# Windowed attention and a SoLU layer on one core: another order for the opening, two weight blocks' remainders on GpSimd, and the last tile evicted by one engine

## The chip, the core and the metric

The kernel runs on one core of a Trainium2 chip. The metric is device time in microseconds. A core has these engines: TensorE (PE, with its weight loads shown apart as PEld), VectorE (DVE), ScalarE (ACT), GpSimd (POOL) and SyncE (SP), which here only issues DMAs. Each engine works through its own list of instructions in order and waits at semaphores for the others. Matrix products land in PSUM, whose eight banks are one tile here, `banks`.

## What is computed

Attention over 8 batches of 8 heads, 576 positions, 64 wide, with two kinds of masks, and then a layer on the concatenated heads:

```python
mask_plain = (rel >= 0) & (rel < 32)
mask_dil = (rel >= 0) & (rel < 128) & (rel % 4 == 0)
masks = np.stack([mask_plain if h < H // 2 else mask_dil for h in range(H)], axis=0)
scores = np.where(masks[None], scale * (q @ k.T), -1e9)
x = softmax(scores) @ v                       # as 4608 tokens of 512
h = x @ w_in                                  # 512 -> 1024
solu = h * softmax(h)
ln = (solu - mean(solu)) / np.sqrt(var(solu) + 1e-06) * g_ln
out = ln @ w_out                              # 1024 -> 512
```

## The kernel before

**Work.** Attention goes by 32 units n, each two heads of one batch; four units make a batch. The layer goes by 36 tiles i of 128 tokens. Both weights come as 64-bit floating-point numbers and are taken apart on the chip, in 16 blocks b of 128 x 512: blocks 0 to 7 are `w_in` (row group b // 2, column half b % 2), blocks 8 to 15 `w_out`. Every product of the layer is made of three: high part by high part, high part by remainder, remainder by high part.

**Steps.** Each step is a short word with a number. A dictionary at the end of the kernel (`one`) maps words to functions, and the list is the order in which each engine gets its instructions, since scheduling is by hand.

- Loads, all on SP's queue: `q` (one unit's keys and queries, two DMAs), `v` (values), `w` (a block's words, 512 KB, into one of six slots), `i` (the identity, fp32), `ib` (the identity, bf16), `m` (mask), `g` (gains). At most eight loads of a queue are under way: each load waits for the one eight places before it.
- Conversion of block b: `low` and `abs` on ACT (bits out of the words), `sign`, `clamp`, `join` on DVE (the fp32 number), `gain` on ACT (blocks 8 to 15), `hi` on ACT (the rounded high part), and the remainder `lo`. By the letter of `LOW_DIFF` for the block, the remainder is made in one of two ways. With "m" the step `diff` gives TensorE two matmuls of 128 x 512, identity by number and negative identity (`minus`, made once by `neg` on ACT) by high part, and `lo` is a copy by ACT out of PSUM. With "p" `lo` is one subtraction on GpSimd.
- Attention of unit n: `S` (scores on TensorE, for units 0 to 3 with the mask added by a matmul), `mask` (DVE, units from 4 on), `max`, `sub` (DVE for units 0 to 3, GpSimd after), `exp` (ACT), `sum`, `inv`, `norm`, `turn` (DVE), `V` (attend, TensorE), `xh` (ACT spreads the high part into `x_hi`), `xl` (DVE spreads the remainder into `x_lo`; it reads the result of `xh`).
- Layer of tile i: `ha`, `hb`, `hc`, `hd` (24 matmuls of 512 columns into two banks), `peak` (DVE, row maximum), `e` (ACT, exponential), `gate` (DVE, product and row sum), `mid` (centre), `var` (ACT and GpSimd), `t` (transposes on TensorE), `th` (ACT), `tl` (DVE), `o` (24 matmuls), `out` (evict on ACT, store). The two banks of tile i are free for tile i + 1 only after `gate`.

**Order.** `INIT` issues the first loads. `OPENING` is a list written out in words: it interleaves the conversion of all 16 blocks, the first eight units or so and the first tiles. From tile 6 on the fixed list `STEP` takes over. `conv_low` (line 437 of the profile), `conv_abs` (427), `conv_sign` (450), `conv_clamp` (443), `conv_join` (458), `conv_hi` (469), `conv_lo` (482 by ACT, 484 by GpSimd), `spread_hi` (283), `spread_lo` (286), `scores` (191), `attend` (265), `moe_h` (299), `moe_o` (387), `moe_peak` (310) and `moe_gate` (324) are the lines that the rows below name. The last tile is evicted in halves, the left by ACT, the right by DVE (407, 408).

## Time and profile before

| | |
|---|---|
| median of three runs | 567.88 us (567.01 to 571.52) |
| the profiled execution | 567.52 us, of it 565.7 us span of the core's work and 1.8 us around it |
| busy share of the span | PE 94%, PEld 75%, DVE 63%, ACT 42%, POOL 20% |
| mean granted TensorE clock | 0.982 |
| moved by DMA | 51.66 MB, 91 GB/s in the mean |

A row of a timeline gives start, duration (both us), engine, line, operation, written tile <- read tiles, shape and count, and in brackets how long the engine had been idle before it and what ended that. "issue" there means that the profile shows nothing that it waited for. In rows grouped by line the last figures are busy us, mean ns of one, and idle time before with its releaser.

### The profile page before, as it was taken

How to read it: one execution, taken by the hardware profiler on the slowest of the kernel's cores; microseconds unless marked ns; L12 is line 12 of the kernel's file. 1: busy time of each engine (PE TensorE's matmuls, PEld its weight loads, DVE VectorE, ACT ScalarE, POOL GpSimd, SP SyncE). 2: the span in 40 equal slices, each digit the busy share in tenths (PEclk: the TensorE clock that was granted, in tenths of full speed). 3: DMA queues.
4: the chain of work that ended last, by engine and by line, in shares of the span. 5: the costliest groups of instructions: out<-in, count | busy, mean ns of one | idle time of the engine just before them, and what ended most of it. 6: DMA issues, size and time to landing. Idle time of an engine off the chain costs nothing.

```text
span 565.7 us, 16593 instructions
## 1 busy us (share of the span) xinstructions
PE 531.3 (94%) x7424; PEld 422.9 (75%) x7424; DVE 358.2 (63%) x555; ACT 237.3 (42%) x386; POOL 110.6 (20%) x256
## 2 busy tenths in 40 slices
PE   2775799899999999999999999999999999999997
PEld 1443588678888888888888888888888888888885
DVE  2989865576667766567667766567667766533342
ACT  3679754334344333433344333433344333433232
POOL 0002451123112222112112222112112222111111
PEclk9799889899999999999999999999999999999999
DMA  8976102332322233112222222123321000001001
GB/s 304 399 287 237 57 1 93 110 103 93 93 93 92 93 93 93 48 64 93 92 93 93 93 92 93 48 65 93 93 93 48 21 21 21 20 19 38 19 20 37
DMA packets 22103, 51.66 MB, mean 91 GB/s; under 512 B 2704, under 2 KB 3216, under 8 KB 22032
## 3 DMA queue, kind: packets, MB, share of 16 engines
q1 hardware_dynamic: 21888, 50.48, 26.4%
q8 instruction: 58, 0.95, 0.7%
q10 hardware_dynamic: 144, 0.13, 0.1%
q14 instruction: 13, 0.11, 0.1%
HBM read 41.16 MB, written 9.44 MB: 89 GB/s over the span
## 4 chain that ended last, share of the span: by engine, by line
PE 88%; DVE 5%; ACT 3%; issue 2%; DMA 1%; SPq 1%; ACTq 0%
PE banks L299 36%; PE banks L387 36%; PE banks L357 5%; PE banks L265 5%; PE banks L191 5%; DMA id_sb<-ident 1%; DVE x_lo L286 1%; DVE low L450 1%; DVE mag L458 1%; ACT x_hi L283 1%; PE banks L475 1%; DVE mag L443 1%; ACT low L437 0%; ACT w_i L482 0%; DVE nmax L310 0%
## 5 line engine op out<-in xcount | busy, mean ns | idle before, releaser
L299 PE MATMUL banks<-w_i,x_hi 128*128 128x512 f32 x576 | 188.9, 409 | 8.3 <-DVE mu L324 7.7
L387 PE MATMUL banks<-w_o,th 128*128 128x512 f32 x576 | 183.0, 401 | 0.0
L299 PEld LDWEIGHTS banks<-w_i,x_hi 128*128 128x128 f32 x576 | 105.1, 192 | 31.6 <-DVE mu L324 8.1
L387 PEld LDWEIGHTS banks<-w_o,th 128*128 128x128 f32 x576 | 107.0, 189 | 23.9
L299 PE MATMUL banks<-w_i,x_lo 128*128 128x512 f32 x288 | 115.0, 399 | 0.6 <-DVE x_lo L286 0.5
L387 PE MATMUL banks<-w_o,tl 128*128 128x512 f32 x288 | 112.8, 395 | 0.0
L310 DVE TENSOR_REDUCE nmax<-banks 128x1 f32<-128x1024 f32 x36 | 44.1, 1224 | 66.9 <-PE banks L299 66.9
L230 ACT ACTIVATE sm<-sm 128x640 f32<-128x640 f32 x32 | 23.5, 737 | 132.0 <-POOL sm L226 128.6
L317 ACT ACTIVATE e<-banks,nmax 128x1024 f32<-128x1024 f32 x36 | 40.2, 1117 | 65.9 <-DVE nmax L310 62.9
L372 DVE TENSOR_TENSOR tl<-banks,th 128x512 fp32r<-128x512 f32 x72 | 46.4, 685 | 32.3 <-ACT th L364 32.3
L299 PEld LDWEIGHTS banks<-w_i,x_lo 128*128 128x128 f32 x288 | 55.1, 191 | 14.3 <-DVE x_lo L286 1.4
L226 POOL TENSOR_TENSOR sm<-sm,mx 128x640 f32<-128x640 f32 x28 | 35.4, 1263 | 151.0 <-DVE mx L217 150.9
L387 PEld LDWEIGHTS banks<-w_o,tl 128*128 128x128 f32 x288 | 54.5, 189 | 12.8
L341 ACT ACTIVATE e<-t 128x1024 f32<-128x1024 f32 x36 | 38.2, 1061 | 49.6 <-DVE t L336 49.5
L205 DVE TENSOR_TENSOR sm<-banks,mask_sb 128x640 f32<-128x640 f32 x28 | 23.1, 824 | 54.5 <-PE banks L191 54.4
L364 ACT CAST th<-banks 128x512 fp32r<-128x512 f32 x72 | 38.8, 590 | 36.8 <-PE banks L357 36.7
L324 DVE CUSTOM_DVE_ANT_0 t<-banks,e 128x1024 f32<-128x1024 f32 x36 | 44.0, 1223 | 15.1 <-ACT e L317 12.0
L265 PEld LDWEIGHTS banks<-pt,vt 32*64 32x64 f32 x2816 | 33.8, 130 | 16.8 <-issue 9.0
L265 PE MATMUL banks<-pt,vt 32*64 32x64 f32 (+3 forms) x2816 | 37.3, 227 | 4.7 <-DVE pt L249 3.6
L191 PEld LDWEIGHTS banks<-kt,qt 64*32 64x32 f32 x2560 | 29.0, 109 | 15.0 <-issue 14.2
L357 PE MATMUL banks<-id_sb,t 128*128 128x128 f32 x288 | 37.5, 273 | 0.5 <-DVE x_lo L286 0.5
L357 PEld LDWEIGHTS banks<-id_sb,t 128*128 128x128 f32 x288 | 33.6, 141 | 5.8 <-DVE x_lo L286 0.8
(54 smaller groups left out, 469.5 us busy)
## 6 DMA issues: line engine op xcount, KB each, us to landing
vt<-vw SPq DMA_DIRECT2D x32, 384.0 KB, 3.6
kt<-kT SPq DMA_DIRECT2D x32, 312.0 KB, 3.1
qt<-qT SPq DMA_DIRECT2D x32, 296.0 KB, 4.1
out<-ob SPq DMA_DIRECT2D x35, 256.0 KB, 2.0
t<-w_in SPq DMA_DIRECT2D x6, 512.0 KB, 6.8
t<-w_out SPq DMA_DIRECT2D x4, 512.0 KB, 6.8
raw<-w_out SPq DMA_DIRECT2D x4, 512.0 KB, 4.7
raw<-w_in SPq DMA_DIRECT2D x2, 512.0 KB, 8.4
```

Of the source, the lines that this page charges most:

```text
L191: nc.tensor.matmul(out=ps_s[WIN * c : WIN * c + WIN, h, WQ * i : WQ * i + WQ], lhsT=qt[D * h : D * h + D, q0 : q0 + WIN], rhs=kt[D * h : D ...
L226: eng.tensor_tensor(out=st[n]["sm"], in0=st[n]["sm"], in1=wide(mx), op=ALU.subtract)
L265: nc.tensor.matmul(out=ps_x[D * h : D * h + D, c, c0 : c0 + k1 - k0], lhsT=vt[WIN * c : WIN * c + WIN, i, D * h : D * h + D], rhs=pt[WIN * ...
L299: nc.tensor.matmul(out=ps_h[:, half, :], lhsT=a[:, kt, xs], rhs=w_i[:, kt, half, part, :], start=(kt == 0 and k == 0), stop=(kt == KT - 1 ...
L310: nc.vector.tensor_reduce(out=nmax, in_=h, axis=AX.X, op=ALU.max, negate=True)
L317: nc.scalar.activation(out=e, in_=h, func=AF.Exp, bias=nmax, scale=1.0, accum_out=se)
L324: nc.vector.tensor_tensor_reduce(out=t, in0=h, in1=ms[i]["e"], scale=1.0, scalar=0.0, op0=ALU.mult, op1=ALU.add, accum_out=mu,)
L341: nc.scalar.activation(out=e, in_=t, func=AF.Square, accum_out=sq)
L357: nc.tensor.transpose(out=ps[:, f, :], in_=ms[i]["t"][:, k * P : k * P + P], identity=id_sb)
L364: nc.scalar.copy(out=th[:, 4 * c : 4 * c + 4], in_=ps_t[c].rearrange("p (f q) -> p f q", q=P))
L372: nc.vector.tensor_tensor(out=tl[:, fs], in0=ps_t[c].rearrange("p (f q) -> p f q", q=P), in1=ms[i]["th"][:, fs].bitcast(F32), op=ALU.subtract,
L387: nc.tensor.matmul(out=ps_o if i < NTILE - 1 else ps_last, lhsT=a[:, f, :], rhs=w_o[:, f, part, :], start=k == 0, stop=k == 3 * FT - 1,)
```

## The change

Four things. The opening's two lists are others: the words of block 0 are the first load, the negative identity is taken after the first block's high part, and nearly every later step stands elsewhere. The mask is loaded in two halves, plain first, dilated later. Blocks 6 and 7 make their remainders on GpSimd, no longer on TensorE and ACT. The last tile is evicted by one ACT instruction of 512 columns; the two stores remain.

```diff
-LOW_DIFF = 'mmmmmmmmpppppppp'
+LOW_DIFF = 'mmmmmmpppppppppp'
-INIT = "q0 ib m w0 w1 v0 i g q1 w2 w3 v1 q2 w4 w5 v2 q3 v3"
+INIT = "w0 q0 ib m0 i w1 v0 q1 w2 w3 v1 m1 q2 w4 w5 v2 g q3 v3"
 OPENING = (
-    "neg0 S0 q4 max0 low0 abs0 sign0 clamp0 low1 sub0 abs1 join0 w6 exp0 "
...
+    "low0 abs0 sign0 clamp0 join0 w6 S0 q4 hi0 neg0 max0 low1 sub0 abs1 "
...
-        left, right = ob[:, :m], ob[:, m:]
-        nc.scalar.activation(out=left, in_=ps_last[:, :m], func=AF.Copy, scale=ms[i]["rstd"])
-        nc.vector.tensor_scalar(
-            out=right, in0=ps_last[:, m:], scalar1=ms[i]["rstd"], scalar2=None, op0=ALU.mult
-        )
-        nc.scalar.dma_start(out=out[rows, :m], in_=left)
-        nc.sync.dma_start(out=out[rows, m:], in_=right)
+        nc.scalar.activation(out=ob, in_=ps_last, func=AF.Copy, scale=ms[i]["rstd"])
+        nc.scalar.dma_start(out=out[rows, :m], in_=ob[:, :m])
+        nc.sync.dma_start(out=out[rows, m:], in_=ob[:, m:])
...
-        "m": lambda _: nc.sync.dma_start(out=mask_sb, in_=mask),
+        "m": lambda d: nc.sync.dma_start(out=mask_sb[:, d], in_=mask[:, d]),
```

SP's queue at the very start, before; `t0` and `t1` are the slots of the words of blocks 0 and 1, `id_sb` the fp32 identity:

```order
L141 DMA kt0_93<-kT 128x624
L142 DMA qt0_92<-qT 128x592
L497 DMA id_bf_82<-ident_bf 128x128
L499 DMA mask_sb_80<-mask 128x640
L169 DMA t0_98<-w_in 128x1024
L169 DMA t1_100<-w_in 128x1024
L149 DMA vt0_102<-vw 128x768
L496 DMA id_sb_78<-ident 128x128
```

The same place after the change:

```order
L169 DMA t0_92<-w_in 128x1024
L141 DMA kt0_95<-kT 128x624
L142 DMA qt0_94<-qT 128x592
L493 DMA id_bf_82<-ident_bf 128x128
L495 DMA mask_sb_80<-mask 128x320
L492 DMA id_sb_78<-ident 128x128
L169 DMA t1_101<-w_in 128x1024
L149 DMA vt0_103<-vw 128x768
```

The words of block 0 moved from the fifth place to the first, the identity from the eighth to the sixth, and the mask is half as long.

ACT in the middle of the opening, around the `low` of block 7 (`t1`, second use of that slot), before; `raw4`, `raw5`, `t0` are words of blocks 4, 5 and 6, casts into `w_i` are `hi` (from `mag`) or `lo` (from `banks`), a cast into `x_hi` is `xh`:

```order
L437 ACTIVATE low1_399<-raw5_122,below_84 128x512
L482 CAST w_i_85<-banks_89 128x512
L427 ACTIVATE mag1_406<-raw5_122 128x512
L482 CAST w_i_85<-banks_89 128x512
L469 CAST w_i_85<-mag0_391 128x512
L230 ACTIVATE sm0_464<-sm0_464 128x640
L283 CAST x_hi_87<-banks_89 128x576
L437 ACTIVATE low2_473<-t0_194,below_84 128x512
L427 ACTIVATE mag2_476<-t0_194 128x512
L437 ACTIVATE low3_486<-t1_251,below_84 128x512
```

After:

```order
L465 CAST w_i_85<-mag2_269 128x512
L283 CAST x_hi_87<-banks_89 128x576
L433 ACTIVATE low3_407<-t1_250,below_84 128x512
L423 ACTIVATE mag3_410<-t1_250 128x512
L465 CAST w_i_85<-mag1_294 128x512
L283 CAST x_hi_87<-banks_89 128x576
L230 ACTIVATE sm1_470<-sm1_470 128x640
L465 CAST w_i_85<-mag0_300 128x512
L478 CAST w_i_85<-banks_89 128x512
L433 ACTIVATE low2_533<-t0_140,below_84 128x512
```

Block 7 (`low3`) is now taken before block 6 (`low2`), and before the second unit's `xh`, block 4's `hi` and the third exponential, which all stood ahead of it.

TensorE at the second output (`moe_o`, the rows with `w_o`), before; `pt` and `vt` are an attend block, `kt` and `qt` a scores block, `x_hi` and `x_lo` the layer's first product:

```order
L387 MATMUL banks_89<-w_o_86,tl1_1017 128x512
L265 MATMUL banks_89<-pt1_1094,vt1_462 64x32 x8
L265 MATMUL banks_89<-pt1_1094,vt1_462 64x64 x24
L265 MATMUL banks_89<-pt1_1094,vt1_462 64x48 x8
L265 MATMUL banks_89<-pt1_1094,vt1_462 64x16 x8
L191 MATMUL banks_89<-kt2_378,qt2_377 32x64 x40
L299 MATMUL banks_89<-w_i_85,x_hi_87 128x512 x2
```

After, between the first output and the second:

```order
L265 MATMUL banks_89<-pt1_1133,vt1_463 64x32 x8
L265 MATMUL banks_89<-pt1_1133,vt1_463 64x64 x24
L265 MATMUL banks_89<-pt1_1133,vt1_463 64x48 x8
L265 MATMUL banks_89<-pt1_1133,vt1_463 64x16 x8
L299 MATMUL banks_89<-w_i_85,x_hi_87 128x512 x2
L299 MATMUL banks_89<-w_i_85,x_lo_88 128x512
L299 MATMUL banks_89<-w_i_85,x_hi_87 128x512 x2
L299 MATMUL banks_89<-w_i_85,x_lo_88 128x512
L191 MATMUL banks_89<-kt3_400,qt3_399 32x64 x40
```

Where attend and scores stood one behind the other, two sets of three wide matmuls stand between them. Earlier, in the wait for the first tile's `gate`, the scores of units 4 and 5 now stand together ahead of all matmuls of tile 1; before, one of them stood amid these.

## The prediction

> **What bounds the kernel now.** The page says TensorE, but as a mean; so I read busy time by stage, then the timeline of each engine over the opening.

> ```profile
> 10.00:33.00 23.00, 16.35 (x377) 9.68 (x376) 20.36 (x39) 17.52 (x30) 0.00 (x0) 0.85 1.03 401
> 33.00:52.20 19.20, 14.06 (x352) 8.69 (x350) 17.85 (x29) 15.16 (x25) 2.20 (x2) 1.00 0.67 235
> 52.20:70.00 17.80, 10.10 (x113) 7.80 (x112) 15.14 (x24) 14.51 (x25) 7.35 (x10) 0.81 0.33 102
> 96.90:110.00 13.10, 11.13 (x215) 8.84 (x219) 8.20 (x13) 3.16 (x5) 1.91 (x4) 0.87 0.30 101
> 126.70:552.00 425.30, 425.25 (x5676) 344.48 (x5675) 263.34 (x399) 160.71 (x263) 83.37 (x206) 1.00 0.21 67
> ```

> Columns: stretch, length, busy time of PE, PEld, DVE, ACT and POOL, then TensorE's clock, DMA share, GB/s. From 126.7 us on PE is full, and the change touches nothing there but the last eviction. So only the first 126.7 us can move, and they move the end one for one. In them the bound changes: 10 to 33 is DMA at 401 GB/s with DVE close behind, 33 to 52 is DVE (17.85 of 19.2), and from 52 on the chain of the first tiles through DVE and ACT, then PE.

> **The early start.** w0 to w15 are the weight blocks' words.

> ```profile
> 2.56 0.91 SPq L169 DMA_DIRECT2D t<-w_in  x2
> 10.40 0.31 ACT L500 ACTIVATE minus<-id_sb 128x128 fp32r<-128x128 f32 x1 [8.40 <-DMA id_sb<-ident]
> 11.38 0.69 DVE L450 SCALAR_TENSOR_TENSOR low<-t,low 128x512 int32<-128x512 int32 x1 [3.59 <-ACT low L437]
> 22.12 0.33 SPq L169 DMA_DIRECT2D t<-w_in  x1
> 30.70 0.64 ACT L283 CAST x_hi<-banks 128x576 fp32r<-128x576 f32 x1
> 32.45 0.75 ACT L437 ACTIVATE low<-t,below 128x512 int32<-128x512 uint16 x1
> 33.11 0.65 ACT L427 ACTIVATE mag<-t 128x512 f32<-128x512 f32 x1
> 35.45 0.62 ACT L469 CAST w_i<-mag 128x512 fp32r<-128x512 f32 x1 [0.39 <-DVE mag L458]
> ```

> The DMA issues of single moments, with the time to landing last (those at 2.56 and 22.12):

> ```profile
> t<-w_in SPq DMA_DIRECT2D x1, 512.0 KB, 5.2
> t<-w_in SPq DMA_DIRECT2D x1, 512.0 KB, 8.5
> ```

> w0 lies there at 2.56 + 5.2 = 7.8, but ACT, in order, stands at the negation until the identity lands, so DVE's first conversion starts at 11.4. First in the queue, w0 should land near 4, and ACT and DVE get through block 0 before 9: about 2.9 us of DVE work sooner. S0 in turn waits for the mask and the queries behind 512 KB more, about 2 us later; the wait told next swallows that.

> I do not credit those 2.9 us, because the words of block 7 do not come sooner. w7 lands at 22.12 + 8.5 = 30.6. The bytes ahead of it are the same before and after (the identity, masks and gains only change places, w6 and w7 keep theirs behind the same loads), and the queue is saturated. Now `low7` starts at 32.45, 1.85 us behind its data, with 29 ACT instructions done. The new list has it after 23. At the 0.76 us each that ACT took for those 29 from 10.4 on, 23 take 17.5 us: it is there at 27.9 if ACT starts no sooner than now, at 21.5 if it starts near 4. **ACT then stands in front of w7 until about 30.6**, and behind it are abs7, hi5 and xh1: 0.75 + 0.65 + 0.62 + 0.64, less some 0.1 each since neighbours overlap (32.45 + 0.75 against 33.11): 2.4 us, so xh1 is done at 33.05. DVE's next instruction after sub3 is xl1, which reads xh1's result. DVE has 34 instructions ahead of xl1; at the rate of its 38 from 11.38 to 32.94 they are done by 30.7 even from today's start. So it waits, whatever the start won.

> **The first tile's peak (peak0).** DVE's groups from 10 to 52.2, then rows of the timeline:

> ```profile
> L458 DVE SCALAR_TENSOR_TENSOR mag<-mag,low 128x512 int32<-128x512 int32 x11 | 7.3, 673 | 0.0
> L450 DVE SCALAR_TENSOR_TENSOR low<-t,low 128x512 int32<-128x512 int32 x8 | 5.4, 674 | 3.6 <-ACT low L437 3.6
> L234 DVE TENSOR_REDUCE rs<-sm 128x10 f32<-128x640 f32 x4 | 3.2, 811 | 1.0 <-ACT sm L230 1.0
> L239 DVE RECIPROCAL rs<-rs 128x10 f32<-128x10 f32 x4 | 0.9, 217 | 0.1
> L238 DVE TENSOR_SCALAR rs<-rs 128x10 f32<-128x10 f32 x4 | 0.7, 165 | 0.0
> ```

> ```profile
> 31.37 0.76 DVE L286 TENSOR_TENSOR x_lo<-banks,x_hi 128x576 fp32r<-128x576 f32 x1
> 32.94 0.82 DVE L244 TENSOR_TENSOR sm<-sm,rs 128x640 f32<-128x640 f32 x1
> 49.66 1.74 POOL L484 TENSOR_TENSOR w_o<-mag,w_o 128x512 fp32r<-128x512 f32 x1 [49.24 <-ACT w_o L469]
> 50.14 1.55 DVE L443 TENSOR_SCALAR mag<-mag 128x512 f32<-128x512 f32 x1
> 52.21 1.21 DVE L310 TENSOR_REDUCE nmax<-banks 128x1 f32<-128x1024 f32 x1
> 54.54 0.41 DVE L443 TENSOR_SCALAR mag<-mag 128x512 f32<-128x512 f32 x1
> ```

> At 32.94 DVE has behind it, beyond what the new list has at 33.05: xl1 0.76, sign6 0.67, sum2 0.81 and inv2 0.38, some 2.4 us with neighbours' overlap. The new list also puts join9 before peak0 (now just behind it): 0.6. From 33.0 to 52.2 DVE is busy 17.85, of which 1.1 is the clamp at 50.14 that a POOL subtraction held (1.55 against 0.41). So 17.85 - 1.1 + 2.4 + 0.6 = 19.75 us of work, plus what POOL costs. Blocks 6 and 7 now subtract on POOL, like the one at 49.66: between nothing and 1.1 us of DVE each; lo6 stands beside norm2 and sign7, lo7 beside two clamps, so I take 0.8 + 1.1. Other waits: 0 to 1.35 (today's idle); I take none. **peak0 starts at 33.05 + 21.65 = 54.7, 2.5 later than now.** The four matmuls and two ACT copies that the two blocks lose stand in a stage where PE has 5 us to spare: nothing.

> [...]

> **From peak0 to the second gate.**

> ```profile
> 51.17 1.04 PE L191 MATMUL banks<-kt,qt 64*32 64x64 f32 x80
> 56.15 1.22 PE L299 MATMUL banks<-w_i,x_hi 128*128 128x512 f32 x2 [3.94 <-DVE mu L324]
> 61.38 1.04 PE L191 MATMUL banks<-kt,qt 64*32 64x64 f32 x80
> 65.21 1.03 PE L357 MATMUL banks<-id_sb,t 128*128 128x128 f32 x8
> 70.03 0.73 PE L299 MATMUL banks<-w_i,x_hi 128*128 128x512 f32 x2 [3.79 <-DVE mu L324]
> ```

> Now this takes 17.8 us (52.2 to 70.0): 3.9 to gate0, 9.1 for tile 1's matmuls with a scores block (61.38) among them, 4.8 to gate1. The new list has both scores blocks, S4 and S5, in the wait for gate0, so 1.0 leaves. The clock in this stage is 0.81 on average, worst after the idle 3.94; two blocks in the gap shorten the idle stretches to about two and one. All of the slow part is worth some 2.4 us, bounds 0 to 2.4; I take 0.9, as S5 still waits for mask4 behind peak0. **1.9 us back.** I go no higher also because ACT's queue between e0 and e1 holds four low, four abs and two hi (6.9 us by the rows above) beside the tile's own work.

> **From there to PE's full stage.**

> ```profile
> 38.44 0.38 PE L191 MATMUL banks<-kt,qt 64*32 64x64 f32 x18 [1.32 <-issue]
> 98.08 0.90 PE L191 MATMUL banks<-kt,qt 64*32 64x64 f32 x69
> 100.94 0.33 PE L191 MATMUL banks<-kt,qt 64*32 64x64 f32 x11 [1.97 <-issue]
> 114.20 1.08 PE L265 MATMUL banks<-pt,vt 32*64 32x64 f32 x80 [0.64 <-DVE x_lo L286]
> 117.83 0.66 PE L357 MATMUL banks<-id_sb,t 128*128 128x128 f32 x4 [0.51 <-DVE x_lo L286]
> ```

> At 98.98 PE stops inside a scores block for 1.97 us with no releaser, and then works below full clock: 0.87 over 13.1 us is 1.7 us lost. The only other such stop, at 37.1, is also in scores directly behind an attend block. I read it as instructions arriving too slowly for two blocks of small matmuls in a row. The new list has at least two sets of three wide matmuls between any attend and the next scores after the first output. So 1.97 + 1.7 go. The waits for x_lo, 1.15, come from attend on the heels of a spread; the new distances should halve them: 0.6. **4.3 us back**, bounds 0 and 4.8.

> **The tail.**

> ```profile
> 562.17 0.47 ACT L407 ACTIVATE ob<-banks,rstd 128x256 f32<-128x256 f32 x1 [3.86 <-PE banks L387]
> 562.68 0.48 DVE L408 TENSOR_SCALAR ob<-banks,rstd 128x256 f32<-128x256 f32 x1 [5.45 <-ACT ob L407]
> 563.19 0.33 SPq L412 DMA_DIRECT2D out<-ob  x1
> ```

> The rows of the tile `ob` (ns, least, median and most):

> ```profile
> L397 ACT ACTIVATE ob<-banks,rstd x35: 688/703/706, 83.9 to 556.6; 128x512 f32<-128x512 f32 x35
> ```

> The halves run one after the other. One ACT instruction of 512 columns takes 0.70 us in the 35 other tiles, so the last DMA goes out at 562.9, where the one at 563.19 stands now: **0.3 back**.

> **Sum.** 2.5 - 1.9 - 4.3 - 0.3 = -4.0 on the profiled execution's 567.52 (span 565.7): **563.5**. The median of the runs is 567.88, within 0.4 of it.

> **Rivals.** One stop remains: if the spacing does not feed PE, a stop with its slow clock, 3.7, stays, and 567.2 results. Two stops, the slower side: PE's order past the first output is attend, two sets, scores, two sets, attend, two sets, scores, each block of 80 records or more; if supply falls short there as it does at 98.98, it stops in both scores blocks, 7.4 against today's 3.7, and nothing of the 4.3 is left: with 2.5 - 1.9 - 0.3 and one stop more, 571.5. Against it speaks the full stage, which has an attend and a scores block for most tiles and lost 0.05 us in 425.30. Third, the change does what it says all the way, and w7 does not hold ACT: DVE goes on near 28 and keeps its lead, up to 5 us better, 558.5. Against it stand the equal bytes and the 401 GB/s. Fourth, PE stays at full clock through gate0's gap: 1.5 more than I took, 562.

> [...] The stop of 1.97 us with a slow clock behind it disagrees, hence its low chance.

> **How the numbers follow.** Forecast 0.50, one stop 0.18, two stops 0.12, no hold at w7 0.10, full clock 0.10. The range 558.5 to 569.5 takes in the bounds of POOL (0 to 2.2), w7's landing (0.7 either way) and idle (1.35), and of the rivals all but the slowest. A change under 1% (562.2 to 573.6) is about what a measurement here can't tell from none. A third of the forecast's own spread (0.17), all of the third rival and 0.07 of the fourth lie below 562.2; of two stops a quarter (0.03) lies above 573.6, and 0.04 more is room for a wait that I have not seen.

> **What would show it.** In the new profile ACT's `low7` follows an idle of 3 us or more, ended by a DMA, near 30.6; DVE idles for 2 to 5 us until 33; peak0 starts near 54.7; both scores blocks lie between it and gate0; no PE idle over 1 us follows the first output. It is wrong if w7 lands before 28, or a stop with no releaser shows after 75 us.

## The result, and the profile after

The median fell from 568.60 us to 565.49 us (17 runs each); the ratio is 0.9949, with a 95% interval of 0.9932 to 0.9966. By the ratio that is 2.9 us (3.1 between the medians), and within the 1% that the prediction called hard to tell from nothing; its number was 563.5. The profiled execution of after took 565.17 us, its span 563.4 (before: 567.52 and 565.7), so the profile shows 2.3 us of it.

Busy time by stage after, with the columns as before (stretch, length, PE, PEld, DVE, ACT, POOL, clock, DMA share, GB/s). The cuts lie at the marks of this run or within 0.2 us of them: first peak, second gate, end of the first output, end of the fourth.

```profile
10.00:33.00 23.00, 14.06 (x395) 8.49 (x394) 17.48 (x33) 14.36 (x24) 0.00 (x0) 0.78 1.03 399
33.00:55.37 22.37, 16.64 (x258) 10.56 (x266) 19.23 (x35) 14.57 (x23) 3.27 (x3) 0.77 0.60 200
55.37:70.68 15.31, 8.61 (x192) 6.89 (x190) 13.89 (x21) 14.42 (x26) 9.53 (x11) 1.00 0.35 112
70.68:84.40 13.72, 13.72 (x56) 10.92 (x56) 11.74 (x16) 8.49 (x15) 9.31 (x14) 0.88 0.01 1
84.40:123.46 39.06, 38.24 (x730) 30.76 (x730) 26.82 (x45) 16.55 (x24) 7.04 (x15) 1.00 0.38 111
```

The first peak comes at 55.37 (52.21 before), the second gate ends at 70.63 (69.97), the fourth output ends at 123.6 (126.9), the fifth starts at 132.84 (135.34). After that the two run alike to the last tile. So the opening up to the second gate lost 0.7 us, and the stage behind it won nearly all.

Rows of the timeline of after at the places that the prediction names:

```profile
5.27 1.28 ACT L433 ACT_TABLE_LOAD   x1 [5.27 <-DMA t<-w_in]
7.35 0.69 DVE L446 SCALAR_TENSOR_TENSOR low<-t,low 128x512 int32<-128x512 int32 x1 [6.47 <-ACT low L433]
28.82 0.37 PE L191 MATMUL banks<-kt,qt 64*32 64x64 f32 x2 [3.23 <-issue]
29.22 0.82 DVE L217 TENSOR_REDUCE mx<-banks 128x10 f32<-128x640 f32 x1 [3.28 <-PE banks L191]
29.85 0.77 ACT L433 ACTIVATE low<-t,below 128x512 int32<-128x512 uint16 x1 [5.55 <-DMA t<-w_in]
32.25 0.76 DVE L286 TENSOR_TENSOR x_lo<-banks,x_hi 128x576 fp32r<-128x576 f32 x1 [1.14 <-ACT x_hi L283]
33.39 1.08 PE L191 MATMUL banks<-kt,qt 64*32 64x64 f32 x52 [0.94 <-issue]
55.37 1.23 DVE L310 TENSOR_REDUCE nmax<-banks 128x1 f32<-128x1024 f32 x1
57.38 1.04 PE L191 MATMUL banks<-kt,qt 64*32 64x64 f32 x80 [1.08 <-DVE sm L205]
59.37 0.72 PE L299 MATMUL banks<-w_i,x_hi 128*128 128x512 f32 x2 [0.96 <-DVE mu L324]
70.68 1.17 PE L299 MATMUL banks<-w_i,x_hi 128*128 128x512 f32 x2 [4.67 <-DVE mu L324]
91.56 0.32 PE L265 MATMUL banks<-pt,vt 32*64 32x16 f32 x13 [0.82 <-issue]
132.47 0.44 PE L265 MATMUL banks<-pt,vt 32*64 32x48 f32 x29 [0.48 <-issue]
559.71 0.69 ACT L406 ACTIVATE ob<-banks,rstd 128x512 f32<-128x512 f32 x1 [3.85 <-PE banks L387]
560.42 0.33 SPq L408 DMA_DIRECT2D out<-ob  x1
560.42 0.37 ACTq L407 DMA_DIRECT2D out<-ob  x1
```

The first thing to see is the two places where DVE and ACT stand. ACT waits 5.55 us for w7 (29.85), as forecast. But DVE had already been standing since 25.9, because TensorE stopped two matmuls short of the end of the scores S3, with no releaser (28.82). The second: stops of that kind are still there, at 33.39, 91.56 and 132.47, though none of these three as long as the 1.97 before. The third: the wait for the first gate is now two idle stretches of 1.08 and 0.96, and the clock in that stage is 1.00 (0.81 before). Four questions follow: what the stops are, what held DVE in the opening, what the shorter waits are worth, and which of the parts brought the 2.9 us.

### The profile page after: what moved, and what is told of

Same layout as the page of the kernel before. It is cut to its first block, busy times and chain, and to the rows that moved or that the text cites. A ratio compares the mean times of both kernels' runs of the same rounds, so it can differ in the third digit from the quotient of the medians.

```text
span 563.4 us, 16573 instructions
## 1 busy us (share of the span) xinstructions
PE 528.9 (94%) x7418; PEld 421.2 (75%) x7418; DVE 358.6 (64%) x554; ACT 236.2 (42%) x384; POOL 113.3 (20%) x258
## 4 chain that ended last, share of the span: by engine, by line
PE 91%; DVE 3%; DMA 3%; ACT 1%; issue 1%; SPq 0%; ACTq 0%
PE banks L387 37%; PE banks L299 36%; PE banks L357 6%; PE banks L265 6%; PE banks L191 5%; DMA t<-w_in 1%; PE banks L471 1%; DMA vt<-vw 1%; DMA mask_sb<-mask 1%; DVE nmax L310 0%; DVE x_lo L286 0%; DVE t L324 0%; PE banks L183 0%; ACT w_i L478 0%; DVE mag L454 0%
## 5 line engine op out<-in xcount | busy, mean ns | idle before, releaser
L299 PE MATMUL banks<-w_i,x_hi 128*128 128x512 f32 x576 | 187.9, 407 | 5.9 <-DVE mu L324 5.6
L387 PE MATMUL banks<-w_o,th 128*128 128x512 f32 x576 | 182.3, 400 | 0.0
L299 PEld LDWEIGHTS banks<-w_i,x_hi 128*128 128x128 f32 x576 | 104.8, 191 | 30.4 <-DVE mu L324 6.2
L387 PEld LDWEIGHTS banks<-w_o,th 128*128 128x128 f32 x576 | 106.3, 188 | 23.5
L299 PE MATMUL banks<-w_i,x_lo 128*128 128x512 f32 x288 | 114.1, 396 | 0.0
L387 PE MATMUL banks<-w_o,tl 128*128 128x512 f32 x288 | 112.5, 395 | 0.0
L310 DVE TENSOR_REDUCE nmax<-banks 128x1 f32<-128x1024 f32 x36 | 44.0, 1223 | 60.9 <-PE banks L299 60.8
L230 ACT ACTIVATE sm<-sm 128x640 f32<-128x640 f32 x32 | 23.6, 737 | 125.5 <-POOL sm L226 125.5
L299 PEld LDWEIGHTS banks<-w_i,x_lo 128*128 128x128 f32 x288 | 54.7, 190 | 12.7
L387 PEld LDWEIGHTS banks<-w_o,tl 128*128 128x128 f32 x288 | 54.2, 188 | 12.7
L324 DVE CUSTOM_DVE_ANT_0 t<-banks,e 128x1024 f32<-128x1024 f32 x36 | 44.0, 1223 | 14.5 <-ACT e L317 11.6
L265 PEld LDWEIGHTS banks<-pt,vt 32*64 32x64 f32 x2816 | 34.3, 133 | 19.1 <-issue 11.9
L265 PE MATMUL banks<-pt,vt 32*64 32x64 f32 (+3 forms) x2816 | 37.9, 230 | 7.2 <-ACT w_i L478 3.3
L191 PEld LDWEIGHTS banks<-kt,qt 64*32 64x32 f32 x2560 | 29.4, 110 | 17.5 <-issue 15.5
L191 PE MATMUL banks<-kt,qt 64*32 64x64 f32 x2560 | 35.3, 235 | 5.3 <-issue 4.2
L286 DVE TENSOR_TENSOR x_lo<-banks,x_hi 128x576 fp32r<-128x576 f32 x32 | 31.5, 984 | 11.5 <-ACT x_hi L283 11.5
## 6 DMA issues: line engine op xcount, KB each, us to landing
t<-w_in SPq DMA_DIRECT2D x6, 512.0 KB, 6.1
t<-w_out SPq DMA_DIRECT2D x4, 512.0 KB, 6.2
raw<-w_out SPq DMA_DIRECT2D x4, 512.0 KB, 5.5
raw<-w_in SPq DMA_DIRECT2D x2, 512.0 KB, 9.0
```

The lines of the kernel that those rows point to most:

```text
L191: nc.tensor.matmul(out=ps_s[WIN * c : WIN * c + WIN, h, WQ * i : WQ * i + WQ], lhsT=qt[D * h : D * h + D, q0 : q0 + WIN], rhs=kt[D * h : D ...
L265: nc.tensor.matmul(out=ps_x[D * h : D * h + D, c, c0 : c0 + k1 - k0], lhsT=vt[WIN * c : WIN * c + WIN, i, D * h : D * h + D], rhs=pt[WIN * ...
L299: nc.tensor.matmul(out=ps_h[:, half, :], lhsT=a[:, kt, xs], rhs=w_i[:, kt, half, part, :], start=(kt == 0 and k == 0), stop=(kt == KT - 1 ...
L310: nc.vector.tensor_reduce(out=nmax, in_=h, axis=AX.X, op=ALU.max, negate=True)
L324: nc.vector.tensor_tensor_reduce(out=t, in0=h, in1=ms[i]["e"], scale=1.0, scalar=0.0, op0=ALU.mult, op1=ALU.add, accum_out=mu,)
L387: nc.tensor.matmul(out=ps_o if i < NTILE - 1 else ps_last, lhsT=a[:, f, :], rhs=w_o[:, f, part, :], start=k == 0, stop=k == 3 * FT - 1,)
```

## Experiments: single parts put into the kernel before

Each of the four has one edit to the kernel before. The groups of four ran each beside the kernel before on one chip, and their ratios are to that.

**Attend and scores apart.**

```diff
-    "V5 v9 out1 S6 q10 turn7 xh5 xl5 hb3 mask6 max6 o2 peak3 sub6 "
+    "V5 v9 out1 hb3 S6 q10 turn7 xh5 xl5 mask6 max6 o2 peak3 sub6 "
```

> The kernel before, with hb3 (six wide matmuls) moved ahead of S6, so that V5 and S6 no longer stand one behind the other; nothing else differs. Theory (the stop of 1.97 us and the slow clock behind it come from two blocks of small matmuls in a row): no stop over 0.5 us between 90 and 105, clock 1.00 there, and 2.5 to 3.7 us less than before. Rival A (the stop belongs to the stage and moves): a stop of 1 us or more in S6 or V5 all the same, and within 1 us of before. Rival B (stop goes but the slow clock of 96.9 to 110 has another cause): 1.5 to 2.0 less.

Measured: ratio 0.9959 (0.9935 to 0.9983), 2.3 us less; the medians lie only 0.7 apart, so the size is loose. Clock in the stretch 96.9 to 110, and TensorE's timeline there:

```profile
96.90:110.00 13.10, 11.72 (x291) 9.02 (x290) 7.86 (x13) 4.22 (x7) 1.91 (x4) 1.00 0.31 101
101.66 0.35 PE L191 MATMUL banks<-kt,qt 64*32 64x64 f32 x17 [0.40 <-issue]
103.00 0.72 PE L387 MATMUL banks<-w_o,th 128*128 128x512 f32 x2 [0.98 <-DVE sm L205]
```

The stop shrank from 1.97 to 0.40 and the clock stayed up. A new wait of 0.98 came in its place, since the output now follows the scores directly and needs their bank. From the second gate to the fifth output the run takes 63.75 us, against 65.37: 1.6 less in the trace. One detail shows more than the length. The stop now leaves 17 matmuls of the block behind it, where it left 11. Six matmuls were moved ahead of the block, so **the stop stayed at the same place in TensorE's list of instructions** and the block moved past it.

**The second scores block into the wait for the first gate.**

```diff
-gain11 abs12 S5 q9 join9 ... low14 mask5 mid0 ... max5 S4 q8
+gain11 abs12 S5 q9 mask5 S4 join9 ... low14 mid0 ... max5 q8
```

> The kernel before, with mask5 and S4 right behind S5, so that both scores blocks stand in the wait for gate0; nothing else differs. Theory (1.0 us of matmuls leaves the path, and the shorter idle keeps the clock up): second gate 1.9 us sooner after peak0 than the 17.8 of before, end 1.5 to 2.4 less. Rival A (DVE and ACT bound gate1, PE only waits longer there): gate1 less than 0.7 sooner, end within 0.7 of before. Rival B (mask5 between peak0 and gate0 delays the gate by its 0.9 us): end 0 to 0.9 more.

Measured: ratio 1.0002 (0.9979 to 1.0025). TensorE's timeline and two windows of this run, then the same windows of before:

```profile
53.97 1.24 PE L191 MATMUL banks<-kt,qt 64*32 64x64 f32 x80 [1.97 <-DVE sm L205]
56.65 0.83 PE L299 MATMUL banks<-w_i,x_hi 128*128 128x512 f32 x2 [1.44 <-DVE mu L324]
68.67 1.22 PE L299 MATMUL banks<-w_i,x_hi 128*128 128x512 f32 x2 [3.79 <-DVE mu L324]
66.00:68.00 2.00, 0.00 (x0) 0.00 (x0) 2.00 (x4) 1.75 (x4) 0.00 (x0) 0.85 0.00 0
68.00:74.20 6.20, 5.53 (x13) 4.38 (x14) 3.20 (x7) 4.95 (x9) 4.66 (x6) 0.50 0.00 0
```

```profile
66.00:68.00 2.00, 0.24 (x3) 0.00 (x1) 2.00 (x5) 2.00 (x4) 0.00 (x0) 1.00 0.09 36
68.00:74.20 6.20, 4.17 (x12) 3.32 (x13) 4.57 (x9) 4.71 (x9) 4.01 (x3) 0.77 0.00 0
```

The second gate comes 16.64 us behind the peak (17.76 before), so 1.1 us was won. From there to the first output it takes 9.01 us (8.05), so 1.0 was given back: the next wait is as long as before (3.79), but the clock falls while it lasts and stays at 0.50 for some 6.8 us, where before it was down for 3.4.

**The first block's words first.** The first loads and the first fourteen steps as after, all else as before.

```diff
-INIT = "q0 ib m w0 w1 v0 i g q1 w2 w3 v1 q2 w4 w5 v2 q3 v3"
+INIT = "w0 q0 ib m0 i w1 v0 q1 w2 w3 v1 m1 q2 w4 w5 v2 g q3 v3"
-    "neg0 S0 q4 max0 low0 abs0 sign0 clamp0 low1 sub0 abs1 join0 w6 exp0 "
+    "low0 abs0 sign0 clamp0 join0 w6 S0 q4 hi0 neg0 max0 low1 sub0 abs1 exp0 "
```

> The kernel before, with the first loads and the first fifteen steps of the list after it (the words of block 0 loaded first, the mask in halves, the negative identity later); all later steps as before. Theory (DMA bounds it: the words of block 7 do not come sooner): DVE starts 4 us sooner, but low7, today 1.85 us behind its data, takes no more than those; peak0 and end 1.0 to 1.9 less. Rival A (the lead is carried): end 2.9 less or more. Rival B (something between takes it, DVE waits elsewhere): end within 0.7 of before.

Measured: ratio 0.9987 (0.9965 to 1.0008). The lead is not carried. At the first unit's row sum behind the early steps it is still 2.75 us (27.87 against 30.62), at the fourth scores it is 1.6, at the first peak 0.8. The largest single loss, 1.1 of the 2.75, is at a stop again:

```profile
36.82 0.35 PE L191 MATMUL banks<-kt,qt 64*32 64x64 f32 x17 [2.45 <-issue]
37.27 0.82 DVE L217 TENSOR_REDUCE mx<-banks 128x10 f32<-128x640 f32 x1 [1.86 <-PE banks L191]
```

Before, the same stop at the same place took 1.32 us (the 38.44 row of the prediction). TensorE got there sooner and stood longer.

**Blocks 6 and 7 on GpSimd.**

```diff
-LOW_DIFF = 'mmmmmmmmpppppppp'
+LOW_DIFF = 'mmmmmmpppppppppp'
```

(and the two `diff` steps left out of the list)

> The kernel before, with the remainders of blocks 6 and 7 made by GpSimd (four matmuls and two ACT copies less); nothing else differs. Theory of the prediction (GpSimd's subtractions hold DVE 0.8 to 1.1 us each, the freed PE and ACT time is worth nothing): peak0 and end 1 to 2 more. Rival A (little contention, as the trace of after showed): within 0.7 of before. Rival B (the freed ACT time counts): 0.7 to 1.5 less.

Measured: ratio 1.0033 (1.0006 to 1.0061), 1.9 us more. Rows of the timeline:

```profile
36.76 1.35 POOL L484 TENSOR_TENSOR w_i<-mag,w_i 128x512 fp32r<-128x512 f32 x1 [36.34 <-ACT w_i L469]
36.89 2.38 DVE L458 SCALAR_TENSOR_TENSOR mag<-mag,low 128x512 int32<-128x512 int32 x2
90.10 0.66 PE L265 MATMUL banks<-pt,vt 32*64 32x64 f32 x39 [1.62 <-issue]
104.35 0.31 PE L191 MATMUL banks<-kt,qt 64*32 64x64 f32 x5 [2.11 <-issue]
```

One subtraction held DVE: two joins that took 1.28 us before took 2.38, so 1.1. The other (40.00 to 41.30) stood beside DVE work that took what it always takes. And the stop in S6 now leaves 5 matmuls, not 11, and a new one of 1.62 us stands in V4. Six matmul records had been taken out ahead of both. That is a third sign that the stops sit in the list, not in a kind of block.

By their ratios the four parts come to about -1 us together (-2.3, +0.1, -0.7 and +1.9, each with 1.2 to 1.6 either way), where the whole change gave -2.9. What is missing lies within these intervals or in the new order of all the other steps, which no run here takes apart.

## What the stops are

The trace has TensorE's matmul records complete, so they can be counted. The page's list of DMA queues has one that moves instructions, for before:

```profile
q8 instruction: 58, 0.95, 0.7%
```

That is 58 transfers, each of 16384 bytes; TensorE has 7424 matmuls and as many weight loads. If these transfers bring them, that makes 256 instructions or 128 matmuls for one transfer. The trace of before has 74 more instructions on TensorE's lists (semaphores, drains), 1.3 for each transfer. If they are among the 256, the matmuls of one transfer are a little fewer than 128: (256 - 1.3) / 2 = 127.4, an estimate from these counts. The start and end of these transfers, read from the trace beside the record at which each stop ends (times in us from the span's start):

```
run                    record   record 127      transfer        work goes on   behind the
                                earlier starts  start to end                   transfer's end
before                   603      35.07         35.89  37.00       38.44          1.44
before                  1367      97.35         98.22  99.53      100.94          1.41
after                    349      22.77         26.22  27.34       28.82          1.48
after                    477      28.88         31.00  32.03       33.39          1.36
after                   1241      87.55         89.18  90.14       91.56          1.42
after                   1877     128.74        129.75 131.12      132.47          1.35
hb3 ahead of S6         1367      98.10         98.94 100.26      101.66          1.40
6 and 7 on GpSimd       1113      86.78         87.18  88.84       90.10          1.26
6 and 7 on GpSimd       1367     100.60        101.62 102.92      104.35          1.43
S3 ahead of V0 (below)   349      23.87         27.54  28.64       29.95          1.31
```

Every one of these stops lies at a record that is a multiple of about 127.3 from the others, in every kernel, whatever stands there: 349 in a scores block or an attend, 1113 and 1241 in attends, 603 and 1367 in scores. Each ends 1.3 to 1.5 us after a 16 KB transfer has landed, and that transfer began when TensorE had come to the place 127 records earlier: 0.4 to 2.1 us after it, but 3.4 and 3.7 us after it at record 349. So **a piece of 127 records that ends in one of these stops has taken 3.3 to 4.5 us in all, and 6.0 and 6.1 at record 349.** Loads ran at 401 GB/s ahead of record 349 in after, but at 393 ahead of record 477 too, so the loads alone do not settle the length. Nor is 3.3 a floor: where the transfer had begun within 0.6 us of the piece's start, pieces of 2.1 to 2.4 us stopped as well (record 1113 with the second scores block moved and with the first words first, record 1877 with blocks 6 and 7 on GpSimd). Eighty small matmuls take 1.04 us, so a piece with little else in it stops at its end for the rest. Wide matmuls (0.23 us each) are what gives a piece its time. A piece can pass faster where its transfer began ahead: behind a stretch of wide matmuls in before, one began at 131.46 for a record that starts at 133.25, and the 127 went by in 1.47 us without a stop. What decides how far ahead it is asked for, the runs do not say. That the stops wait for these transfers is read from times, not from a releaser, but the ten rows do not stand alone: the fourteen traces hold 41 stops over 0.2 us without a releaser, each lies at one of eight such records (222, 349, 477, 604, 1113, 1241, 1368, 1877, give or take one), the transfers come in the order of these pieces, and each stop ends 1.2 to 1.6 us behind the end of its transfer.

## Experiments: what held DVE in the opening

Three changes to the kernel after, and one of two of them together. After itself was not run beside these four, and its ratio was 0.9949 and 0.9967 in the two groups that have it; so what each change does is read from its trace, and its ratio, which is to before, gives no verdict against after.

**S3 ahead of V0.**

```diff
-... lo3 abs4 inv1 V0 v4 sign5 hi2 norm1 S3 q7 ...
+... lo3 abs4 inv1 S3 V0 v4 sign5 hi2 norm1 q7 ...
```

> The kernel after, with S3 ahead of V0 on TensorE, nothing else on any engine's order (a load of values moves by a place). In after, S3 stops for 3.23 us two matmuls before its end, at TensorE's record 349. Theory A (instructions come in pieces of 127 matmul records, the next piece only about 3.4 us after the one before has been entered, more under DMA load; a stop lies where the piece ends, whatever stands there): no stop inside S3, the stop at record 349 to 351 now at the end of V0 or start of V1 and shorter, max3 near 26 in place of 29.2. Rival A' (a scores block directly behind an attend stops): no stop at 349 at all. Theory B (ACT stands at w7's words and holds xh1): xl1 stays at 32.3 and peak0 within 0.5 of 55.4, end within 0.7 of after. Rival B' (the stop of S3 held DVE): peak0 and end 2 to 3 less.

Measured: ratio 0.9994 (0.9970 to 1.0018). TensorE's timeline and DVE's:

```profile
29.95 0.29 PE L265 MATMUL banks<-pt,vt 32*64 32x16 f32 x2 [3.72 <-issue]
30.95 0.76 DVE L286 TENSOR_TENSOR x_lo<-banks,x_hi 128x576 fp32r<-128x576 f32 x1 [6.21 <-ACT x_hi L283]
```

The stop is at record 349 again, now two matmuls short of the end of V0, and not shorter. V0's result is wanted sooner than S3's was, so DVE stands 6.21 us, and the first peak comes at 57.4. Theory A holds for the place and was wrong on the length; that w7 would bind and leave the peak alone (B) was wrong too.

**low7 and abs7 behind the third exponential.**

```diff
-... turn1 low7 xl0 abs7 join5 ... norm3 exp2 sign6 ...
+... turn1 xl0 join5 ... norm3 exp2 low7 abs7 sign6 ...
```

> The kernel after, with low7 and abs7 behind the third exponential (exp2) in ACT's order, nothing else moved. Theory (two holds lie side by side, w7's words on ACT and the stop in S3, which also holds V1 until 30.8): xl1 at 31.5 in place of 32.25, peak0 and end 0.3 to 1.0 less. Rival A (w7's hold alone bounds): xl1 near 28, end 3 to 4 less. Rival B (w7's later conversion is late for the first tile): end 0.5 to 2 more.

Measured: ratio 0.9989 (0.9964 to 1.0014). x_lo of the second unit starts at 31.70 (32.25 in after), the first peak at 55.31 (55.37). With ACT free of w7, V1 still waits behind the stop:

```profile
29.00 0.37 PE L191 MATMUL banks<-kt,qt 64*32 64x64 f32 x2 [3.09 <-issue]
31.70 0.76 DVE L286 TENSOR_TENSOR x_lo<-banks,x_hi 128x576 fp32r<-128x576 f32 x1 [0.40 <-ACT x_hi L283]
```

So the two holds lie side by side, and the w7 hold is worth half a microsecond beyond the other; that half is gone again by the peak.

**Both, and the last tile in two tiles.** The eviction as before, but the left half into `ob` and the right half into the free tile `e`.

> The kernel after, with both: S3 ahead of V0, and low7 and abs7 behind exp2; beside that the last tile evicted in halves by ACT and DVE into two different tiles. Theory (with both holds gone DVE goes on): xl1 near 28 in place of 32.25, peak0 2 to 4 less than 55.4, and that much of the end if no later wait takes it (TensorE's clock and gate1's chain are such waits). Rival (later waits, blocks 4 and 12 to 15, take it back before gate1): gate1 within 0.7 of 70.7 and end within 0.7 of after. Tail: both evictions start within 0.1 us of each other and last 0.47 each; from the last matmul's end to the span's end 0.2 less than the 3.86 of after, rival 0.

Measured: ratio 1.0013 (0.9991 to 1.0035). The stop at 349 lies in V0 again (3.76 us), and the first peak comes at 57.1: moved, not removed. At the tail:

```profile
561.34 0.47 ACT L407 ACTIVATE ob<-banks,rstd 128x256 f32<-128x256 f32 x1 [3.85 <-PE banks L387]
561.84 0.49 DVE L408 TENSOR_SCALAR e<-banks,rstd 128x256 f32<-128x256 f32 x1 [5.44 <-ACT ob L407]
```

DVE still starts when ACT is done, with two written tiles as with one. It is not the written tile that makes it wait; both still read `banks` and the same `rstd`, and which of these it is was not tested. From the last matmul's end to the span's end it is 3.79 us here, 3.86 after, 3.73 before.

**w7 sooner.** S3 ahead of V0, and 1600 KB of loads behind w10.

```diff
-... w6 S0 q4 ... S1 q5 join1 w7 ... V0 v4 ... join4 w10 ...
+... w6 S0 ... S1 join1 w7 ... S3 V0 ... join4 w10 q4 q5 v4 ...
```

> The kernel after, with S3 ahead of V0, and the loads of units 4 and 5 (queries and keys) and of values 4 moved behind the words of block 10; ACT's, DVE's and TensorE's orders as in after otherwise. 1216 KB less lie ahead of w7 at 400 GB/s. Theory (DMA's queue sets when w7 lands, and w7 holds ACT): w7 lands and low7 starts 2 to 3 us sooner than 29.85, xl1 as much, peak0 2 to 3 less, the later words too. Rival A (the limit of eight loads under way or the slots set it): low7 within 0.7 of 29.85. Rival B (w7 sooner, but a later wait takes it back): peak0 sooner by 2, gate1 and end within 0.7 of after.

Measured: ratio 0.9998 (0.9976 to 1.0020). w7's load is issued at 19.2 in place of 22.4, and ACT no longer waits for it at all:

```profile
29.98 0.64 ACT L283 CAST x_hi<-banks 128x576 fp32r<-128x576 f32 x1 [6.65 <-PE banks L265]
30.52 0.76 ACT L433 ACTIVATE low<-t,below 128x512 int32<-128x512 uint16 x1
```

The first peak comes at 56.6 all the same: 0.8 sooner than with S3 ahead of V0 alone (57.4), but 1.2 later than in after. The stop at record 349 holds V0 until 29.66 here. So in this order TensorE's instructions bind where the words no longer do. Two runs were not tried: w7 sooner with S3 in its old place, and fewer TensorE records ahead of S3, which would push record 349 behind its end.

## Experiments: after once more, and two versions meant to beat it

**After itself.**

> The kernel after itself, unchanged, beside the three that follow. If the stops lie at fixed places of TensorE's instruction stream and their lengths follow from when the next piece is asked for: stops inside scores and attend blocks end at records 349, 477, 1241 and 1877 again, each within 0.6 us of 3.2, 0.9, 0.8 and 0.5. Ratio to before between 0.993 and 0.999.

Measured: ratio 0.9967 (0.9949 to 0.9985). The stops are at the same records (349, 477, 1241, 1877), 3.80, 0.95, 0.59 and 0.23 us long. But the span of this profiled execution is 566.3, and 2.6 us of the difference to the other one arise at one place:

```profile
55.00:70.70 15.70, 10.63 (x141) 8.21 (x124) 11.65 (x18) 12.73 (x22) 9.34 (x11) 0.78 0.38 116
57.21 1.07 PE L191 MATMUL banks<-kt,qt 64*32 64x64 f32 x80 [1.91 <-DVE sm L205]
59.21 1.22 PE L299 MATMUL banks<-w_i,x_hi 128*128 128x512 f32 x2 [0.93 <-DVE mu L324]
```

The wait between the two scores is 1.91 here and was 1.08. The clock fell (0.78 against 1.00 over this stage), and the second gate comes 13.9 us behind the first, not 11.3. The same program falls on either side from one execution to the next. The clock had come back from an earlier fall at 51.27 here and at 53.69 in the other, so the first tile's matmuls ran faster here, the scores ahead of the wait ended 1.0 us sooner (55.31 against 56.30), and what TensorE then waits for on DVE did not come sooner. Five profiles have this order up to the first gate: in two (after, and the last version below) this wait is 1.1 us and the clock holds, in three (this one and the next two versions) it is 1.9 and the clock falls. TensorE was not idle all the time before the fall: from 54.7 to about 58.1, where the clock fell, it worked some 1.5 us, on small matmuls, and the one idle stretch in it is the 1.91.

**Attend and scores side by side.**

```diff
-... mask6 V5 v9 max6 hd3 xh5 sub6 ...
+... mask6 hd3 V5 v9 max6 xh5 sub6 ...
-... tl4 hb5 S9 q13 hd5 mask9 ...
+... tl4 S9 q13 hb5 hd5 mask9 ...
```

> The kernel after, with hd3 (six wide matmuls) moved ahead of V5, so that V5 and S7 stand one directly behind the other, and with S9 moved ahead of hb5, so that twelve wide matmuls stand between S9 and V8 in place of six; nothing else moves on TensorE. Theory (a piece of 127 records with under about 3.4 us of work in it stops at its end, and what stands side by side does not matter): from record 1113 to 1240 lie now 4.3 us of work, so no stop over 0.2 us at 1240, none in the adjacent V5 and S7, none at 1877; from gate1 on 1.0 to 1.3 us less than after. Rival (the prediction's rule: a scores block directly behind an attend stops): a stop of 1 to 2 us in S7, and from gate1 on 0 to 1 more than after.

Measured: ratio 0.9957 (0.9934 to 0.9981). V5 and S7 are the first two rows:

```profile
94.84 1.21 PE L265 MATMUL banks<-pt,vt 32*64 32x32 f32 x96
95.97 1.04 PE L191 MATMUL banks<-kt,qt 64*32 64x64 f32 x80
96.94 0.72 PE L299 MATMUL banks<-w_i,x_hi 128*128 128x512 f32 x2
84.00:123.00 39.00, 39.00 (x734) 31.30 (x733) 27.07 (x44) 17.39 (x26) 7.03 (x15) 1.00 0.38 111
```

No bracket: an attend with a scores block on its heels runs through without a stop. Record 1240 still lies in V5, but twelve wide matmuls now stand in the piece that ends there. The stops at 1241 and 1877 are gone, and TensorE is busy for all of 39.0 us. From the first output to the fifth it takes 52.44 us, against 54.19 and 53.72 in the two profiles of after. The prediction's reading, two blocks of small matmuls in a row, is refuted as a rule; the count of the piece is what decides. In the runs' times the loss of the two stops does not show: this ratio is within the interval of after's on the same chip (0.9967).

**TensorE kept at work in the wait for the second gate.**

```diff
+    def keep_warm(_):
+        for k in range(16):
+            nc.tensor.matmul(
+                out=ps_o, lhsT=minus, rhs=w_i[:, 0, 0, 0, :], start=True, stop=True
+            )
```

(and its step in the list, `warm0`, behind `hb1`)

> The kernel after, with 16 matmuls added on TensorE behind hb1, in the wait for gate1 (negative identity by the first weight block, into a bank that is free there; their result is never read); nothing else moves. Theory (the 1.7 us that the first matmuls of tile 2 lose is the clock falling after the 4.67 us of idle, and keeping TensorE at work holds it): clock 1.00 from 70.7 to 74.2 in place of 0.69 and 0.50, the first output starts 1.3 to 1.7 us sooner behind gate1 than the 8.0 of after, and so does everything after it. Rival A (the clock falls all the same): no change. Rival B (DVE's second half of block 12 to 15 or the gains are late then): less than 0.7.

Measured: ratio 0.9935 (0.9912 to 0.9958).

```profile
68.65 3.90 PE L413 MATMUL banks<-w_i,minus 128*128 128x512 f32 x16
73.48 0.73 PE L299 MATMUL banks<-w_i,x_hi 128*128 128x512 f32 x2 [0.93 <-DVE mu L324]
70.70:74.20 3.50, 2.57 (x11) 1.77 (x11) 3.50 (x9) 3.11 (x7) 0.56 (x1) 1.00 0.00 0
```

Tile 2 runs at full clock from its first matmuls on (two in 0.73 us, where after took 1.17), and the first output starts 6.43 us behind the second gate, against 8.02 and 8.96. The span of this execution is 563.9 although its first gap fell on the slow side (0.78 from 55 to 70.7, as in after once more). The theory holds: that much of the stage was the clock, and work that nobody reads buys it back. The stop at 1241 is there as expected, 0.90 long.

**Both, and the second gate sooner.** The two edits above, and `gate1` moved ahead of `join14`.

> The kernel after, with both (hd3 ahead of V5, S9 ahead of hb5; the 16 added matmuls in the wait for gate1), and with gate1 one DVE instruction earlier, ahead of join14. Theory: 0.6 at gate1, 1.3 to 1.7 by the clock, 1.0 to 1.3 by the two stops: 2.9 to 3.6 us less than after, so a ratio to before near 0.990. Rival (the opening's spread from run to run, about 1.5 us at the first peak, hides it; or the gains and block 14's later number are late): within 1 us of after.

Measured: ratio 0.9935 (0.9912 to 0.9958), the profiled execution 562.01, its span 560.2. In it no stop is left behind the first peak. From the first gate's end to the second's it takes 10.7 us (11.3 in after), but two waits came back:

```profile
79.46 0.50 PE L387 MATMUL banks<-w_o,th 128*128 128x512 f32 x1 [0.29 <-POOL w_o L486]
84.03 0.73 PE L299 MATMUL banks<-w_i,x_hi 128*128 128x512 f32 x2 [0.62 <-DVE mu L324]
```

Block 14's number is later, its remainder on GpSimd holds the first output, and the third gate holds tile 3. So whether the earlier gate gains anything in the end is open: the ratio is that of the 16 matmuls alone. Against before, this version and the one with the 16 matmuls alone are 3.7 us faster (0.65% of 567.7). On the same chip after itself is 1.9 faster (0.33%). The intervals of after and of these two overlap, so that they beat before is shown, and that they beat after is likely. The two edits without the earlier gate were not tried.

## Why the prediction was right, and where it was not

- **Sum.** 4.0 us were forecast; 2.3 were found in the profile, 2.9 by the ratio of the runs. By the marks of the two profiles: +0.7 up to the second gate (forecast +0.6), -3.9 from there to the end of the fourth output (-4.3), +0.7 from there to the start of the fifth (0), and in the tail +0.1 from the start of ACT's eviction to the end (-0.3). That the first of these agrees is luck: it is +3.2 at the first peak (forecast +2.5) and -2.5 behind it (-1.9), and the second of these came in two of five executions, as told below.
- **Its own signs.** As it said, no idle of TensorE over 1 us followed the first output. But it had named a stop with no releaser after 75 us as a sign of being wrong, and two came, 0.82 at 91.56 and 0.48 at 132.47.
- **Early start not credited.** Right, and with one part alone too: 4.0 us sooner at DVE (7.35 against 11.38), 0.7 us at the end, within 0 by its interval. w0 landed at 5.27, not near 4, and ACT's table load (1.28) now stands behind it. The reason given was only half of it: w7 does hold ACT from 24.3 to 29.85, but TensorE's stop at record 349 holds DVE over the same time. With w7 off ACT's path the peak does not move (55.31); with w7 asked for 3 us sooner and S3 ahead of V0 it comes at 56.6.
- **xh1 done at 33.05, first peak at 54.7.** It was done at 32.2, and the peak came at 55.37 (54.8 to 55.5 in the four other profiles with this order up to there). Two terms were off and largely cancel. "Other waits: I take none" failed: DVE stood 3.1 us between 33.0 and the peak, 1.07 and 1.42 of it in two waits for ACT. And DVE's work in that stretch was 19.2 us where 21.65 had been added up. GpSimd's price, taken as 1.9, was about 0.5 here: two clamps in 1.24 us, where three took 1.09 later in the same profile. With the part alone it was 1.1 for one subtraction and nothing for the other, so both bounds were met, at different places.
- **From the first peak to the second gate, 1.9 us back.** 2.5 in the profile of after. The fourth rival, full clock through this gap, is what that execution shows; after once more, it takes 17.9 us from peak to gate, which is 2.6 longer and no gain at all (before: 17.8). Over the five profiles with this order it took 15.3 us in after and 14.7 in the last version, where the clock held (in the last version with the gate one instruction earlier), and 17.9 to 18.1 where it fell. The term "all of the slow part is worth some 2.4 us" was the right size; but 0.9 of it was taken as a mean, and each of the five executions got nearly all of it or none; their waits differ by some 0.8 us (1.1 and 1.9). The part alone, in the kernel before, gained 1.1 at the gate and lost it to the clock in the next wait.
- **4.3 us behind the first output.** 3.9 came. The part alone brought 1.6 in its trace: the stop shrank by 1.57, from 1.97 to 0.40, the clock behind it stayed up as forecast, and a new wait took 0.98. By subtraction (1.62 - 1.57 + 0.98, an estimate) the slow clock was worth some 1.0, where 1.7 had been put down. The cause was named rightly as instructions arriving too slowly and wrongly as two blocks in a row: side by side they run clean when the piece that ends in them holds enough wide matmuls, and six wide ones between them do not help when it does not (0.82 in V5, 0.48 in V8). The rivals of one and two stops were priced by that rule; what came is two small stops without a slow clock.
- **Tail.** Forecast 0.3 back; 3.68 us from the start of ACT's eviction to the end, 3.56 before. One instruction does the work by 560.42, 0.71 us after its start where the last issue before was 1.02 after, so that term was right. But both stores now leave at once and land later: 1.9 and 2.1 us, where they took 1.7 and 1.8 one behind the other, and what follows the issues lasts 2.97 us in place of 2.54. The term left out is this landing.

## What to carry to other kernels

Count an engine's instructions, not only its time: where a trace shows stops with no releaser, number the records at which they end, and if the numbers keep one distance, spread the long instructions so that no piece is passed in less time than the next takes to arrive. A lead won at the start is worth nothing until every engine's supply, data and instructions both, has been looked at. And where the first matmuls behind a wait run at half clock (0.50 here), work that is thrown away in the wait can pay: here it brought the next stage 1.6 to 2.5 us sooner.
